# The key cache read in eight 4 MB transfers instead of sixteen 2 MB ones, through slots that keys and values share

## The chip, the cores and the metric

The kernel runs on one core of a Trainium2 chip. The metric is device time in microseconds (us), the median of several executions. One further execution is recorded by the hardware profiler; its times are of that one execution.

## The reference

One decode step for four sequences (batch B = 4, one new token each, width 576): a normalised input goes through an attention branch over a sliding window of a key and value cache, and through an MLP branch, and the two results and the input are added.

```python
x = A_x
xn = _layernorm(x)
return x + _A_ref(xn, A_k_cache, A_v_cache, A_wq, A_wo) + _B_ref(xn, B_w1, B_w2, B_w3, B_w4)

def _A_ref(x, k_cache, v_cache, wq, wo):     # caches: (4, 16 kv heads, 8192, 128)
    q = (x @ wq).reshape(B, 1, 32, 128).transpose(0, 2, 1, 3)
    k = repeat(k_cache[:, :, Sk - 2048:, :], 2)   # the last 2048 rows; 2 query heads per kv head
    v = repeat(v_cache[:, :, Sk - 2048:, :], 2)
    p = softmax(einsum("bhqd,bhkd->bhqk", q, k) * 128 ** -0.5)
    return einsum("bhqk,bhkd->bhqd", p, v).reshape(B, 1, 32 * 128) @ wo

def _B_ref(x, w1, w2, w3, w4):               # w1, w2: 576x576; w3: 576x4608; w4: 4608x576
    h = gelu(layernorm(x) @ w1)
    hs = concat(shifted quarters of h) @ w2  # with one token the shifted quarters are zero
    x1 = x + hs
    return x1 + gelu(layernorm(x1) @ w3) @ w4
```

All inputs are bf16. The windows of keys (K) and values (V) are 33.55 MB each; the weights make up the rest of the 88.5 MB that are read.

## The kernel before

**Transfers.** SyncE (SP) issues all large transfers, in the order of their keys, each after its waits (`add_dma`, L205): wq, w1, w2, w3, the first part of w4, then K0 to K15, V0 to V7, the rest of w4, and wo in five pieces. SP waits at the head of its list, so a transfer whose wait is open holds back those behind it.

**Storage.** `kring` holds four slots of 16 KB per partition for K, one 2 MB transfer each (`kslot`). `vring` holds five times 16 KB. V comes in 4 MB transfers; its four slots (`vslot`) are the two halves of `vring`'s first 64 KB and the two halves of `kring`. Before the loops the same memory holds weights: wq in the upper half of `kring`, w3 and the first part of w4 in `vring`. At the end wo goes to `vring`.

**K.** Transfer c brings four kv heads of one sequence, 2048 rows of 128 elements each (`CH`, `kv_src`). The 128 partitions are 32 groups of 64 consecutive rows times 4 heads, the row groups outermost; a partition gets one run of 16 KB. K0 and K1 have no wait, K2 waits for `q` (wq has been used), and from K4 on transfer c waits until TensorE has transposed all of transfer c - 4 (`t_done`).

TensorE runs a loop of `N_LOOP` = 4 turns over `N_CB` = 4 chunks (one chunk is one transfer). A chunk has 8 blocks. For each block `emit_T` (L508) makes eight 128x128 transposes into one of four PSUM buffers, with a permutation `perm_bf` as the moving operand that sorts the columns by head; VectorE or ScalarE copies the buffer to one of 16 `ktb` buffers (L492, L491, five and three of eight blocks). Two blocks into the next chunk, `emit_SC` (L515) makes 16 score matmuls of 512 columns: per matmul the right side is one head's columns of two `ktb` buffers (16 row groups of 32 consecutive elements), the left side a padded block of q (`Qs`, which VectorE copies from `Qpad` for each chunk). All chunks add into the same four PSUM banks `Sps`, [128, 4, 512].

**Between.** After the last chunk: row maximum (L521), exponential (L525), a transpose on VectorE (L543), and 64 small matmuls with selection matrices `pick_bf` (L537) that bring the probabilities into V's order; `mH_bf` spreads them by head (L568).

**V.** Transfer c holds a quarter of the window of two sequences, all 16 heads, in runs of 32 KB per partition with sequence and head outermost (`v_src`). The first MLP output `MO0` (L399, 48 matmuls on w4) stands in V0's list of waits, since `vring` held w3 and w4. V2 and V3 wait for K chunks (`kring` becomes free), and V4 to V7 for the V matmuls of the transfer that used the slot before (`PV`, L576; 64 matmuls per transfer). The last transfer is cut in two halves. The pieces of wo wait for the V matmuls of V4 and V5.

**The end.** The result is normalised, transposed and multiplied by wo piece by piece as it lands (L399), then copied out.

Of the kernel before, what the change touches and what calls it, by code (L numbers as in the profile page):

```python
# [6 lines left out]
BF16 = mybir.dt.bfloat16  # L7
# [7 lines left out]
N_LOOP = 4  # L15
N_CB = 4
# [21 lines left out]
def bass_parallel_sum__sliding_block_cached__mixer_s_mlp__decode_kernel(  # L38
# [8 lines left out]
    NU = 4  # L47
    NC = B * Hkv // NU
    NI = 128 // NU
    NT = W // NI  # L50
    UE = NT * Dh
    NBLK = NT // 8
    NB = NC * NBLK
    LB = N_CB * NBLK
    assert N_LOOP * N_CB == NC and LB % 4 == 0 and LB % NKT == 0
# [6 lines left out]
    CH = [(b, gq) for gq in range(4) for b in range(B)]  # L62
    VCH = [(bp, qt) for bp in range(NPAIR) for qt in range(NVS)]
    NCV, NTV = len(VCH), 2 * NT
# [6 lines left out]
    with ExitStack() as ctx:  # L71
        def sb(name, shape, dt):
            return ctx.enter_context(nc.sbuf_tensor(name, shape, dt))
# [7 lines left out]
        PT_t = sb("PT", [128, NT * 32], BF16)  # L81
# [13 lines left out]
        wot = lambda a, n: vring[:, wo_at(a):wo_at(a) + n * D].rearrange("p (r n) -> p r n", r=n)  # L95
# [39 lines left out]
        Qs = sb("Qs", [128, N_CB, 128], BF16)  # L135
# [46 lines left out]
        for j in range(LB):  # L182
            S["E", j] = sem(f"evac{j}")
# [32 lines left out]
        for n in range(NB):  # L216
            j = n % LB
            ev_val[f"E{n}"] = (("E", j), n // LB + 1 + (j >= LB - 4))
# [26 lines left out]
        pool_ident(permT_bf, "permT_bf", [[-1, NI], [-NI, NU]], permT_bf[:].rearrange("p (i u) -> p i u", u=NU), -93)  # L245
        P(lambda e: e.memset(ktb[:, NKT // 2 * 1024:NKT * 1024], 0.0), key=-92, inc=(("E", LB - 2), 1))  # L246
        P(lambda e: e.memset(Qs[:, N_CB - 1, :], 0.0), key=-91, inc=(("E", LB - 1), 1))
        for j in (LB - 4, LB - 3):
            P(lambda e, j=j: e.sem_inc(S["E", j], 1), key=-90)
# [7 lines left out]
        for gl in range(2):  # L257
            for x in range(2 * NVS):
                v = pick_bf[:, x, gl, 16 * gl:16 * gl + 16].rearrange("p (u r) -> p u r", u=NU)
                P(lambda e, v=v, x=x: e.affine_select(out=v, in_=v, compare_op=ALU.is_equal, fill=0.0, base=-(8 * (x // 2) + x % 2),  # L260
                                                      pattern=[[-NI, NU], [-2, 4]], channel_multiplier=1),
                  waits=["pick11"], sig=f"pick2{gl}{x}", key=-84 + 0.1 * (8 * gl + x))
# [31 lines left out]

        t_done = lambda c: f"T{NBLK * c + NBLK - 1}"
        for c in range(NC):
            w = [t_done(c - N_CB)] if c >= N_CB else (["q"] if c >= 2 else [])
            add_dma([(kslot(c % N_CB), kv_src(A_k_cache, c))], ("k", c % N_CB), w, c)
        for c in range(NCV):
            w = [f"PV{2 * (c - NVS) + 1}"] if c >= NVS else [t_done(NC - N_CB + 2 * c - 3)] if c >= 2 else ["MO0"]  # L300
            for n, (u0, u1) in enumerate([(0, NH), (NH, NTV)] if c == NCV - 1 else [(0, NTV)]):
                add_dma([(vslot(c % NVS)[:, Dh * u0:Dh * u1], v_src(c, u0, u1))], ("v", c % NVS, n), w, KS + c + 0.1 * n)
# [191 lines left out]
        for n in range(NB):  # L494
            c, k = n // NBLK, n % NBLK
            if k == 0:
                add("dve", lambda e, c=c: e.tensor_copy(out=Qs[:, c % N_CB, :], in_=Qpad_t[:, 128 * (4 * CH[c][0] + CH[c][1]):][:, 0:128]),
                    waits=["qT15"] + ([f"SC{c - N_CB}"] if c >= N_CB - 1 else []), key=n)
            eng, f = evac(n)
            w = [f"T{n}"] + ([f"SC{c - 2}"] if c >= 1 else [])  # L500
            add(eng, f, waits=w + (["hT", "hs1", "h2_2"] if n == 0 else []), key=n + 0.2, inc=(("E", n % LB), 1))

        def emit_T(e, j, wait):
            k, kb = j // NBLK, j % NBLK
            wait(j)
            ins = None
            for t in range(8):
                ins = e.transpose(tb[j % 4][:, t, :], kslot_t(k)[:, 8 * kb + t, :], perm_bf[:])  # L508
            ins.then_inc(S["T"], 1)

        def emit_SC(e, k):
            ins = None
            for q in range(4):
                for u in range(NU):
                    ins = e.matmul(Sps[32 * u:32 * u + 32, q, :].rearrange("p (t i) -> p t i", t=16),  # L515
                                   lhsT=Qs[:, k, 32 * u:32 * u + 32], rhs=ktgrp[:, (4 * k + q) % (NKT // 2), :, u, :],
                                   start=False, stop=False, tile_position=(0, 32 * u), skip_group_check=True)
            return ins
# [25 lines left out]
        for qt in range(4):  # L544
# [6 lines left out]
            else:  # L551
# [8 lines left out]
        add("dve", lambda e: e.tensor_copy(out=rinvB[:].rearrange("p (c u e) -> p c u e", u=NU, e=2),  # L560
                                           in_=rinvps.rearrange("p (u c e) -> p c u e", u=NU, e=2)),
# [10 lines left out]
        def emit_PV(e, k, h):  # L572
            ins = None
            for g in range(NH // 2):
                t = NH * h + 2 * g
                ins = e.matmul(ps[:, 0, 0:256], lhsT=PTpad[:, 2 * (k % 2) + h, 2 * g:2 * g + 2].rearrange("p t h e -> p (t h e)"),  # L576
                               rhs=vslot(k)[:, Dh * t:Dh * (t + 2)], start=(k == 0 and t == 0), stop=(k == NVS - 1 and t == NTV - 2),
                               skip_group_check=True)
            ins.then_inc(S["PV"], 1)
# [99 lines left out]
        with nc.Fori(0, N_LOOP, engines=[PE], head_slot={PE: 0}) as it:  # L679
            turn = e.snap(it + 1)  # L680
            landed = e.snap(16 * it + 16)

            def wait(j):
                if j % NBLK == 0:
                    e.wait_ge(S["k", j // NBLK], landed)
                e.wait_ge(S["E", (j - 4) % LB], turn)
            for j in range(LB):
                emit_T(e, j, wait)
                if j % NBLK == 2:
                    k = (j // NBLK - 1) % N_CB  # L690
                    e.wait_ge(S["E", NBLK * k + 6], turn)
                    e.wait_ge(S["E", NBLK * k + 7], turn)
                    emit_SC(e, k).then_inc(S["SC"], 1)
# [50 lines left out]
```

## Time and profile before

| | |
|---|---|
| median of 3 runs | 214.64 us (214.55 to 214.80) |
| span of the profiled execution (first to last instruction) | 213.5 us |
| data read from HBM | 88.49 MB, 415 GB/s over the span |
| TensorE matmuls / weight loads busy | 170.0 / 131.6 us |
| VectorE / ScalarE busy | 119.2 / 59.8 us |
| mean granted TensorE clock | 0.942 |

The profile gives no device time of its own for the profiled execution beside its span; the runs' median is 1.1 us above the span, which is the start and the end outside the first and last instruction. An engine's busy time is a sum over the whole span. Landing times can be read from the chain that ended last, where a DMA piece ends when its transfer has landed, and from TensorE's timeline where a group of matmuls starts after a wait for a DMA.

### The profile page before, as it was taken

To read this page: it belongs to the slowest core of one execution; us is meant where nothing else is said; L and a number is where in the kernel's file an instruction comes from. 1 tells how busy PE (TensorE), PEld (TensorE's weight loads), DVE (VectorE), ACT (ScalarE), POOL (GpSimd) and SP (SyncE) were. 2 spreads that over 40 slices of the span, in tenths; PEclk is the share of its full clock that TensorE was granted. 3 is DMA by queue.
4 is the path that set the end of the run, shared out by engine and by line. 5 is a ranking of instruction groups with operands and counts; after the bars stand their busy time and mean duration, and the time that the engine had idled before them with its cause. 6 is when DMAs were issued, how large, how long until landed. Compare 5 with 4: busy or idle time off the path is not lost.

```text
span 213.5 us, 4894 instructions
## 1 busy us (share of the span) xinstructions
PE 170.0 (80%) x2207; PEld 131.6 (62%) x2211; DVE 119.2 (56%) x185; ACT 59.8 (28%) x72; POOL 16.3 (8%) x39
## 2 busy tenths in 40 slices
PE   2028268579999999999999913899999768599965
PEld 0013115338778888887888702598888658488732
DVE  4973700017776777777677756999674572600110
ACT  2001212005665666666566655100000000000000
POOL 8992000000000000000000000000000000000000
PEclk9999857679999999999999995999999999999999
DMA  7999989999999999999999999999999999999992
GB/s 277 411 380 507 428 369 428 428 430 418 439 414 424 430 433 427 424 436 430 422 424 473 411 448 418 421 461 404 442 424 414 461 411 442 393 436 421 430 417 108
DMA packets 5795, 88.66 MB, mean 415 GB/s; under 512 B 652, under 2 KB 1048, under 8 KB 1816
## 3 DMA queue, kind: packets, MB, share of 16 engines
q1 hardware_dynamic: 5768, 88.49, 97.5%
q8 instruction: 8, 0.13, 0.2%
q14 instruction: 3, 0.02, 0.0%
q10 hardware_dynamic: 16, 0.01, 0.0%
HBM read 88.49 MB, written 0.00 MB: 415 GB/s over the span
## 4 chain that ended last, share of the span: by engine, by line
DMA 47%; PE 44%; DVE 4%; SPq 2%; issue 1%; ACT 1%
PE ps L508 23%; DMA vring<-in_B_w_dram 16%; DMA vring<-in_A_wo_dram 13%; DMA vring<-in_A_v_cache_dram 12%; PE ps L576 10%; DMA kring<-in_A_k_cache_dram 7%; PE ps L515 6%; PE ps L399 3%; SPq L205 2%; DVE vring L543 1%; DVE rmax L521 1%; DVE ktb L568 1%; PE ps L537 1%; ACT ktb L491 0%; PE ps L345 0%
## 5 line engine op out<-in xcount | busy, mean ns | idle before, releaser
L492 DVE COPY ktb<-ps 128x1024 bf16<-128x1024 bf16 x80 | 53.8, 689 | 22.1 <-PE ps L508 22.1
L508 PEld LDWEIGHTS ps<-perm_bf,kring 128*128 128x128 bf16 x1024 | 57.4, 98 | 8.7 <-issue 8.3
L508 PE MATMUL ps<-perm_bf,kring 128*128 128x128 bf16 x1024 | 60.6, 219 | 1.1 <-issue 1.1
L491 ACT ACTIVATE ktb<-ps 128x1024 bf16<-128x1024 bf16 x48 | 47.7, 1023 | 30.2 <-PE ps L508 30.1
L568 DVE TENSOR_TENSOR ktb<-PT,mH_bf 128x4096 bf16<-128x4096 bf16 x16 | 36.2, 2287 | 13.3 <-PE ps L576 13.3
L576 PE MATMUL ps<-vring,ktb 128*128 128x256 bf16 x256 | 28.6, 273 | 4.6 <-DMA vring<-in_A_v_cache_dram 3.8
L576 PE MATMUL ps<-kring,ktb 128*128 128x256 bf16 x256 | 28.6, 273 | 2.6 <-DMA kring<-in_A_v_cache_dram 2.6
L576 PEld LDWEIGHTS ps<-vring,ktb 128*128 128x128 bf16 x256 | 24.8, 98 | 7.9 <-issue 3.6
L576 PEld LDWEIGHTS ps<-kring,ktb 128*128 128x128 bf16 x256 | 25.0, 98 | 6.1 <-issue 2.8
L635 ACT ACTIVATE out_sb<-ps 4x288 bf16<-4x288 f32 x1 | 0.4, 402 | 76.7 <-PE ps L399 76.7
L515 PE MATMUL ps<-ktb,Qs 128*32 128x512 bf16 x272 | 17.8, 382 | 1.2 <-ACT ktb L491 1.2
L335 PE MATMUL ps<-ident_bf,xn_bf 4*128 4x4 bf16 x8 | 0.6, 170 | 11.8 <-DVE xnT L352 9.0
L594 DVE TENSOR_SCALAR tmp<-ps,maskd 128x128 f32<-128x128 f32 x2 | 0.7, 350 | 16.5 <-PE ps L576 16.5
L515 PEld LDWEIGHTS ps<-ktb,Qs 128*32 128x32 bf16 x272 | 5.7, 95 | 6.7 <-DVE ktb L492 1.3
L399 PE MATMUL ps<-vring,h2T_sb 128*4 128x288 bf16 x72 | 7.7, 390 | 2.3 <-DMA vring<-in_B_w_dram 2.3
L537 PE MATMUL ps<-vring,pick_bf 128*32 128x256 bf16 x64 | 3.9, 411 | 6.4 <-DVE rinv L555 6.4
L335 PEld LDWEIGHTS ps<-ident_bf,xn_bf 4*128 4x128 bf16 x8 | 0.4, 112 | 12.8 <-DVE xnT L352 9.1
L325 DVE TENSOR_SCALAR xn_bf<-xn_bf,mv,rstd 4x576 bf16<-4x576 bf16 x1 | 7.5, 7473 | 0.0
L399 PEld LDWEIGHTS ps<-vring,h2T_sb 128*4 128x4 bf16 x72 | 3.9, 110 | 5.6 <-DMA vring<-in_B_w_dram 2.5
L537 PEld LDWEIGHTS ps<-vring,pick_bf 128*32 128x32 bf16 x64 | 2.1, 121 | 8.2 <-DVE rinv L555 6.9
L246 POOL MEMSET ktb<- 128x8192 bf16 x1 | 6.9, 6925 | 0.0
L399 PE MATMUL ps<-vring,ORT 128*4 128x288 bf16 x64 | 4.6, 286 | 2.4 <-DMA vring<-in_A_wo_dram 2.2
(115 smaller groups left out, 84.2 us busy)
## 6 DMA issues: line engine op xcount, KB each, us to landing
kring<-in_A_k_cache_dram SPq DMA_DIRECT2D x16, 2048.0 KB, 13.2
vring<-in_A_v_cache_dram SPq DMA_DIRECT2D x4, 4096.0 KB, 24.5
kring<-in_A_v_cache_dram SPq DMA_DIRECT2D x3, 4096.0 KB, 33.8
vring<-in_B_w_dram SPq DMA_DIRECT2D x1, 4608.0 KB, 24.5
kring<-in_A_wq_dram SPq DMA_DIRECT2D x1, 4096.0 KB, 12.2
kring<-in_A_v_cache_dram SPq DMA_DIRECT2D x2, 2048.0 KB, 27.7
vring<-in_B_w_dram SPq DMA_DIRECT2D x1, 3456.0 KB, 34.4
vring<-in_A_wo_dram SPq DMA_DIRECT2D x1, 1872.0 KB, 30.6
```

Source lines behind the costliest of these rows:

```text
L205: e.dma_start(o_, i_).then_inc(S[skey], 16)
L246: P(lambda e: e.memset(ktb[:, NKT // 2 * 1024:NKT * 1024], 0.0), key=-92, inc=(("E", LB - 2), 1))
L325: add("dve", lambda e: e.tensor_scalar(out=dst[:], in0=src[:], scalar1=mv[:, idx, 0:1], scalar2=rstd[:, idx:idx + 1], op0=ALU.subtract, op ...
L399: return e.matmul(ACC[h], lhsT=lhsT, rhs=rhs, start=start, stop=stop, tile_position=(0, 32 * h), skip_group_check=True)
L491: return "act", lambda e: e.activation(out=ktbuf[:, n % NKT], in_=tb[n % 4], func=ACTF.Copy)
L492: return "dve", lambda e: e.tensor_copy(out=ktbuf[:, n % NKT], in_=tb[n % 4])
L508: ins = e.transpose(tb[j % 4][:, t, :], kslot_t(k)[:, 8 * kb + t, :], perm_bf[:])
L515: ins = e.matmul(Sps[32 * u:32 * u + 32, q, :].rearrange("p (t i) -> p t i", t=16), lhsT=Qs[:, k, 32 * u:32 * u + 32], rhs=ktgrp[:, (4 * k ...
L521: add("dve", lambda e: e.tensor_reduce(out=rmax[:], in_=Sps, axis=AX.XY, op=ALU.max), waits=["SCend"], sig="rmax", key=KS)
L537: ins = e.matmul(ps[32 * j:32 * j + 32, 4 + qt, 256 * ih:256 * (ih + 1)].rearrange("p (t a e) -> p t a e", a=NPAIR, e=2), lhsT=pick_bf[:, ...
L568: return lambda e: e.tensor_tensor(out=PTpad[:, n % 4], in0=PTv[:, qt, NH * h:NH * (h + 1), bp, :].unsqueeze(2).to_broadcast([128, NH, NX, ...
L576: ins = e.matmul(ps[:, 0, 0:256], lhsT=PTpad[:, 2 * (k % 2) + h, 2 * g:2 * g + 2].rearrange("p t h e -> p (t h e)"), rhs=vslot(k)[:, Dh * ...
```

## The change

K comes in eight transfers of 4 MB: eight kv heads of one sequence, 16 row groups of 128 consecutive rows times 8 heads, the row groups outermost, so that a partition gets one run of 32 KB. Four slots of 32 KB per partition (`slot`: the two halves of `kring`, then of `vring`'s first 64 KB) serve K0 to K7 in turn and then V0 to V7. K1 now waits for `q`, K2 for `MO0` (K2 and K3 go into `vring`), K4 to K7 for the transposes of the transfer four before, and V0 to V3 for those of K4 to K7. wo goes to `kring`, where V4 and V5 were.

A chunk is still 8 blocks of transposes and 16 score matmuls, but now half a transfer; the loop has eight chunks and runs twice. Since 32 semaphores (`NE`) for the copies serve 64 blocks of a turn, the value that is waited for changes in the middle of the body. A score matmul takes one head's columns of four `ktb` buffers: 32 row groups of 16 consecutive elements; two banks of `Sps` are written per chunk. `Qs` is copied once per transfer, 256 wide. `perm_bf`, `permT_bf` and `pick_bf` have new patterns for the new order, with the same number of instructions.

```diff
-N_LOOP = 4
-N_CB = 4
+N_LOOP = 2
+N_CB = 8
+NE = 32
...
-    NU = 4
-    NC = B * Hkv // NU
+    NU = 8
+    NCK = B * Hkv // NU
     NI = 128 // NU
     NT = W // NI
-    UE = NT * Dh
-    NBLK = NT // 8
+    NC = 2 * NCK
+    UE = NT * Dh // 2
+    NBLK = NT // 16
...
-    CH = [(b, gq) for gq in range(4) for b in range(B)]
+    CH = [(b, gh) for gh in range(2) for b in range(B)]
...
-        kslot = lambda s: kring[:, s * UE:(s + 1) * UE]
-        kslot_t = lambda s: kslot(s).rearrange("p (t d) -> p t d", t=NT)
-        vslot = lambda k: (vring, vring, kring, kring)[k][:, k % 2 * 2 * UE:(k % 2 + 1) * 2 * UE]
+        slot = lambda k: (kring, kring, vring, vring)[k][:, k % 2 * 2 * UE:(k % 2 + 1) * 2 * UE]
+        slot_t = lambda k: slot(k).rearrange("p (x t d) -> p x t d", x=2, t=NT // 2)
...
-        ktgrp = ktb[:].rearrange("p (s t u i) -> p s t u i", s=NKT // 2, t=16, u=NU)
+        ktgrp = ktb[:].rearrange("p (s t u i) -> p s t u i", s=NKT // 4, t=32, u=NU)
...
-        wot = lambda a, n: vring[:, wo_at(a):wo_at(a) + n * D].rearrange("p (r n) -> p r n", r=n)
+        wot = lambda a, n: kring[:, wo_at(a):wo_at(a) + n * D].rearrange("p (r n) -> p r n", r=n)
...
-        def kv_src(cache, c):
-            b, gq = CH[c]
-            return cache[b, NU * gq:NU * gq + NU, Sk - W:Sk, :].rearrange("g (i t) d -> i g (t d)", t=NT)
+        def k_src(c):
+            b, gh = CH[c]
+            return A_k_cache[b, NU * gh:NU * gh + NU, Sk - W:Sk, :].rearrange("g (i t) d -> i g (t d)", t=NT)
...
-        t_done = lambda c: f"T{NBLK * c + NBLK - 1}"
-        for c in range(NC):
-            w = [t_done(c - N_CB)] if c >= N_CB else (["q"] if c >= 2 else [])
-            add_dma([(kslot(c % N_CB), kv_src(A_k_cache, c))], ("k", c % N_CB), w, c)
+        t_done = lambda c: f"T{2 * NBLK * (c + 1) - 1}"
+        for c in range(NCK):
+            w = [t_done(c - NVS)] if c >= NVS else ([], ["q"], ["MO0"], [])[c]
+            add_dma([(slot(c % NVS), k_src(c))], ("k", c % NVS), w, c)
         for c in range(NCV):
-            w = [f"PV{2 * (c - NVS) + 1}"] if c >= NVS else [t_done(NC - N_CB + 2 * c - 3)] if c >= 2 else ["MO0"]
+            w = [f"PV{2 * (c - NVS) + 1}"] if c >= NVS else [t_done(NCK - NVS + c)]
...
-            if k == 0:
-                add("dve", lambda e, c=c: e.tensor_copy(out=Qs[:, c % N_CB, :], in_=Qpad_t[:, 128 * (4 * CH[c][0] + CH[c][1]):][:, 0:128]),
-                    waits=["qT15"] + ([f"SC{c - N_CB}"] if c >= N_CB - 1 else []), key=n)
+            if k == 0 and c % 2 == 0:
+                add("dve", lambda e, c=c: e.tensor_copy(out=Qs[:, c // 2 % 2, :],
+                                                        in_=Qpad_t[:, 128 * (4 * CH[c // 2][0] + 2 * CH[c // 2][1]):][:, 0:256]),
+                    waits=["qT15"] + ([f"SC{c - 3}"] if c >= 2 else []), key=n)
...
-                ins = e.transpose(tb[j % 4][:, t, :], kslot_t(k)[:, 8 * kb + t, :], perm_bf[:])
+                ins = e.transpose(tb[j % 4][:, t, :], slot_t(k)[:, t % 2, 4 * kb + t // 2, :], perm_bf[:])
...
-            for q in range(4):
-                for u in range(NU):
-                    ins = e.matmul(Sps[32 * u:32 * u + 32, q, :].rearrange("p (t i) -> p t i", t=16),
-                                   lhsT=Qs[:, k, 32 * u:32 * u + 32], rhs=ktgrp[:, (4 * k + q) % (NKT // 2), :, u, :],
+            for q in range(2):
+                for g in range(NU):
+                    u = g % 4
+                    ins = e.matmul(Sps[32 * u:32 * u + 32, 2 * (k % 2) + q, :].rearrange("p (t i) -> p t i", t=32),
+                                   lhsT=Qs[:, k // 2 % 2, 32 * g:32 * g + 32], rhs=ktgrp[:, 2 * (k % 2) + q, :, g, :],
...
         with nc.Fori(0, N_LOOP, engines=[PE], head_slot={PE: 0}) as it:
-            turn = e.snap(it + 1)
+            turn = [e.snap(2 * it + 1), e.snap(2 * it + 2)]
             landed = e.snap(16 * it + 16)
 
             def wait(j):
-                if j % NBLK == 0:
-                    e.wait_ge(S["k", j // NBLK], landed)
-                e.wait_ge(S["E", (j - 4) % LB], turn)
+                if j % (2 * NBLK) == 0:
+                    e.wait_ge(S["k", j // (2 * NBLK)], landed)
+                e.wait_ge(S["E", (j - 4) % NE], turn[j // NE])
```

More of the change, by code (lines that the diff above doesn't have):

```diff
@@ L181, in bass_parallel_sum__sliding_block_cached__mixer_s_mlp__decode_kernel @@
         S["SC"] = sem("score")
-        for j in range(LB):
+        for j in range(NE):
             S["E", j] = sem(f"evac{j}")
@@ L244, in bass_parallel_sum__sliding_block_cached__mixer_s_mlp__decode_kernel @@
         pool_ident(perm_bf, "perm_bf", [[-1, NU], [-NU, NI]], perm_bf[:].rearrange("p (u i) -> p u i", u=NU), -94)
[L245 to L248, printed above, removed]
+        pool_ident(permT_bf, "permT_bf", [[-1, 32], [-32, 4]], permT_bf[:].rearrange("p (i u) -> p i u", u=4), -93)
+        P(lambda e: e.memset(ktb[:, NKT // 2 * 1024:NKT * 1024], 0.0), key=-92, inc=(("E", NE - 2), 1))
+        P(lambda e: e.memset(Qs[:, 1, :], 0.0), key=-91, inc=(("E", NE - 1), 1))
+        for j in (NE - 4, NE - 3):
             P(lambda e, j=j: e.sem_inc(S["E", j], 1), key=-90)
```

38 lines of the change are left out of this document (19 added, 19 removed).

## The prediction

> **What bounds the kernel now.** I read the page first: the engines' busy shares, the row of DMA engines, the queues and the issues.
>
> ```profile
> span 213.5 us, 4894 instructions
> PE 170.0 (80%) x2207; PEld 131.6 (62%) x2211; DVE 119.2 (56%) x185; ACT 59.8 (28%) x72; POOL 16.3 (8%) x39
> DMA  7999989999999999999999999999999999999992
> q1 hardware_dynamic: 5768, 88.49, 97.5%
> q8 instruction: 8, 0.13, 0.2%
> kring<-in_A_k_cache_dram SPq DMA_DIRECT2D x16, 2048.0 KB, 13.2
> ```
>
> No compute engine is full. The 16 DMA engines are: from the second slice to the last but one their row holds nines and one eight, and queue 1, which carries all data, fills 97.5% of 16 engines' span. The time is therefore the time to move 88.5 MB, plus a start and an end. An edit that shortens TensorE's work gains nothing, and one that lengthens it costs nothing until the queue runs dry.
>
> Second, the chain that ended last, in order of time (start, length, what). Its DMA pieces end where a transfer landed.
>
> ```profile
> 5.03 34.43 DMA vring<-in_B_w_dram
> 39.50 5.92 PE ps L399 x48
> ...
> 47.45 1.51 PE ps L508 x24
> 48.97 0.98 PE ps L515 x16
> 49.94 3.71 PE ps L508 x64
> ...
> 103.76 13.99 DMA kring<-in_A_k_cache_dram
> ...
> 122.67 1.03 ACT ktb L491
> ...
> 136.40 7.16 PE ps L576 x64
> ...
> 150.74 25.78 DMA vring<-in_A_v_cache_dram
> 176.52 0.14 issue
> 176.66 7.16 PE ps L576 x64
> 183.82 0.02 issue
> 183.83 27.01 DMA vring<-in_A_wo_dram
> ```
>
> The first w4 part landed at 5.03 + 34.43 = 39.46, the sixteenth K transfer at 103.76 + 13.99 = 117.75, V5 (counted from V0) at 176.52, the wo piece that the chain ends with at 183.83 + 27.01 = 210.84. The PE pieces in between come from waits that link the chain; the transfers queued behind one another kept running under them.
>
> Third, TensorE's timeline where it waits for V, and the windows of the K and V stretches (columns: length, busy time of PE, PEld, DVE, ACT, POOL, clock, DMA share, GB/s).
>
> ```profile
> 166.85 7.16 PE L576 MATMUL ps<-vring,ktb 128*128 128x256 bf16 x64 [1.30 <-DMA vring<-in_A_v_cache_dram]
> ...
> 176.66 7.15 PE L576 MATMUL ps<-vring,ktb 128*128 128x256 bf16 x64 [2.48 <-DMA vring<-in_A_v_cache_dram]
> 186.37 7.15 PE L576 MATMUL ps<-kring,ktb 128*128 128x256 bf16 x64 [2.56 <-DMA kring<-in_A_v_cache_dram]
> ```
>
> ```profile
> 39.46:117.75 78.29, 77.03 (x1251) 62.13 (x1252) 51.57 (x91) 43.97 (x45) 0.00 (x0) 0.96 1.01 428
> 117.75:176.52 58.77, 46.62 (x489) 38.72 (x490) 43.22 (x36) 9.36 (x15) 0.00 (x0) 0.94 1.00 430
> ```
>
> Both stretches have full DMA engines. The K stretch moves sixteen 2 MB transfers in 78.29 us, 4.893 us each, so 9.786 us for 4 MB. The V stretch, 4 MB transfers whose rows are already 32 KB runs, shows what a 4 MB transfer costs: TensorE starts on V5 and V6, each at its landing, at 176.66 and 186.37, 9.71 us apart.
>
> **The transfers.** The bytes stay. K goes from sixteen transfers of 128 rows of 16 KB to eight of 128 rows of 32 KB. If they cost what V's cost, the K stretch is 8 x 9.71 = 77.7 us in place of 78.29: 0.6 us less. The other bound is the 16 KB price kept, nothing gained. I take V's price, the row of exactly this size and run length. The windows' 428 and 430 GB/s point the same way but are too coarse to size it, and the V stretch holds a slip: six V transfers at 9.71 are 58.3 us and it took 58.77.
>
> K's heads lie 8192 x 128 x 2 B = 2 MB apart. With eight heads per transfer two head rows are interleaved more closely than with four; V has its rows of 32 batch-heads outermost, all 2 MB apart, and runs at 430 GB/s all the same. So I charge nothing for the address pattern. [...]
>
> **Whether the queue ever runs dry.** Everything else is free as long as each transfer is issued before the one ahead of it lands; so I follow the schedule, with landings every 9.71 us from 39.46.
>
> - K0 lands at 49.2, K1 at 58.9, K7 at 117.1, V3 at 156.0. Before, K0's 2 MB landed about 44.4 and TensorE, ready at 47.45, did not wait. Now it starts at 49.2.
> - K2 and K3 go into vring, where w3 and w4 stood, and wait for MO0. MO0 ends at 39.50 + 5.92 = 45.4; K0 and K1 keep the engines busy until 58.9, a cover of 13 us. K1 waits for q in SP's queue; w3 and w4 are queued ahead of it, so nothing is short.
> - TensorE needs 3.71 + 0.98 = 4.69 us per 2 MB, 9.4 per 4 MB, less than 9.71: it waits for each K chunk. K4 is issued at 58.6 against 78.3 (K3's landing), V0 when K4 is transposed, about 97 against 117.
> - The last K chunk is now twice as large, so 4.7 us more work follow its landing. Before, from the landing (117.75) to the first V matmul (136.40) was 18.65; now 117.1 + 18.65 + 4.7 = 140.5. The first V is done at 147.6, and only then may V4 be issued. The queue runs dry at 156.0: a cover of 8.4 us, where before it was about 13. V5 to V7 follow at 7.2 us intervals against landings every 9.71, so the cover grows; TensorE has caught up by V5 or V6.
> - The wo pieces go to kring behind V4 and V5 (slots 0 and 1 as before), at about 176 and 183.5; V7 alone fills the engines until 194.8.
>
> So 4.7 us of added TensorE delay at the end of K is hidden under V0 to V3. Eight Qs copies fewer on VectorE, eight issues fewer on SP, other masks on GpSimd: all beside full DMA engines, nothing.
>
> **The score matmuls** read ktb in runs of 16 elements rather than 32. Rows for runs of other lengths:
>
> ```profile
> 123.83 1.05 PE L515 MATMUL ps<-ktb,Qs 128*32 128x512 bf16 x16 [1.21 <-ACT ktb L491]
> 131.29 3.89 PE L537 MATMUL ps<-vring,pick_bf 128*32 128x256 bf16 x64 [6.41 <-DVE rinv L555]
> ```
>
> L515, with runs of 32, takes about 61 ns per 512 columns; L537, with runs of 2, 61 ns per 256. So the bounds are 1 and 2 times. 16 is nearest to 32: I take 1, and the doubling is a rival.
>
> **Instruction fetch.** The K loop's body doubles: 512 transposes and 128 score matmuls, run twice. Queue 8 carries instructions over the same DMA engines; I read it as TensorE's program, since its packets come with the first pass of TensorE's loops.
>
> ```profile
> q1 hardware_dynamic: 2273, 33.47, 100.6%
> q8 instruction: 4, 0.07, 0.3%
> ...
> q1 hardware_dynamic: 1737, 29.67, 100.8%
> q14 instruction: 1, 0.01, 0.0%
> ```
>
> The first pair is the DMA view of 39.46 to 117.75, the second of 67 to 136: four blocks in the loop's first pass or just behind it, none in the three later ones. So a body of 320 matmuls stays resident. The program's matmuls, each counted once, are 2207 less three quarters of L508's 1024 and of 256 of L515's, less half of L576's 512: 991, over 8 blocks, 124 a block. 320 more are two or three blocks. Four blocks in the K stretch took 0.3% of 16 x 78.29 us = 3.8 us of engine time, about 0.9 us each, on one engine. What that costs the whole depends on the engine it meets. A transfer has landed when the last of the engines has done its share, so only a block on the latest engine moves the landings; and the V slip, which came before 166.85, is not made up afterwards (the landings stay 9.71 apart). Four blocks left the K rate even; of the three in the V stretch one may be its slip of 0.5. So 0 to 0.9 us for a block, and I take 0, because most of the 16 engines are not the latest.
>
> **Sum.** -0.6 for the transfers, 0 for all else. The span becomes 212.9. The profiled execution's span is 213.5 and the runs' median 214.64, so 1.1 us lies around the span, which the change leaves: 214.05 us. Telling it from no change needs about 0.2% of this kernel, 0.43 us.
>
> **Rivals.**
>
> 1. An added instruction block meets the DMA engine that is already last: 0.9 us for one, 1.8 for two, less the 0.6. 214.9 to 215.9, and 215.4 in the middle, slower. For it: two or three more blocks, and the V slip shows that such a thing is seen. Against: sixteen engines. The point of decision is one engine. If the longer body (640 matmuls, five blocks by 124 a block) does not stay resident, five more blocks come on the second pass and the chance rises; what TensorE itself would wait, about 0.9 us for a block at the branch, lies under the cover of 8.4. [...] 0.25 together.
> 2. The 16 KB and 32 KB prices are equal for K's address pattern: 214.65, no change. Against it: V's row. 0.13.
> 3. The score matmuls double to 1.95 us per half chunk. TensorE then needs 11.3 us per K chunk, ends K at 139.6 in place of 126, starts V at about 154.3 and V4 is issued at 161.4, 5.4 us after the queue ran dry: 219.4. It decides from about 1.6 us per half chunk. 0.04.
> 4. K's rows, two heads of which are now read at a time, slow one another. Each per cent costs 0.78 us of the K stretch: at 0.8% the gain is gone, at 1.3% the kernel is slower by 0.2%, at 5% it takes 218. V's rate, with more such rows, is against it. 0.03. [...]
>
> That the change does not happen is excluded: SP's list has eight K transfers of 128 x 16384 elements.
>
> **Numbers.** The forecast has 0.55: 214.05, its own range 213.7 (most of the V slip falls on another engine this time) to 214.35 (half of the transfers' gain is lost). Faster by over 0.2% is that case less a little of its upper end: 0.54. Same: rival 2, that end and rival 1's lower edge, 0.16. Slower: the rest of rival 1 and rivals 3 and 4, 0.30. The range 213.7 to 215.6 leaves out rivals 3 and 4 and the top of 1.
>
> **What would show it.** Right: K7 lands near 117.1 and each K landing 9.71 after the last; TensorE's loop shows a wait of 0.3 us per chunk; the first V matmul near 140.5; SP issues V4 near 147.6; V landings stay 9.71 apart; queue 8 has 10 or 11 packets; the last wo lands 0.6 earlier. Wrong: a gap in the row of DMA engines near 156, a score group above 1.6 us, K landings at 9.79 or more, queue 8 with 15 or more packets, or V and wo landings slipping by about 1 us once.

## The result, and the profile after

| | before | after |
|---|---|---|
| median of 4 runs each | 214.72 us (214.55 to 215.79) | 297.88 us (296.63 to 299.10) |
| ratio after / before | | 1.3865, 95% interval 1.3814 to 1.3915 |
| the profiled execution, its span | 214.80 us, 213.5 | 298.05 us, 296.8 |

The changed kernel is 83.2 us slower. The forecast was 214.05 us with a range to 215.6: wrong in sign and by two orders of magnitude in size.

The page of the changed kernel, the rows that answer to those shown of before:

```profile
span 296.8 us, 4864 instructions
PE 188.4 (63%) x2207; PEld 143.3 (48%) x2211; DVE 119.4 (40%) x177; ACT 60.3 (20%) x72; POOL 16.4 (6%) x39
PEclk9998777569579588596695975966958999999999
DMA  8999999999999999999999999999999999999992
GB/s 301 407 455 427 416 233 210 212 205 216 220 212 214 212 214 212 208 219 212 212 212 212 216 218 212 212 243 442 426 424 435 433 423 428 433 417 432 419 419 82
q1 hardware_dynamic: 4616, 88.49, 97.5%
q8 instruction: 11, 0.18, 0.3%
kring<-in_A_k_cache_dram SPq DMA_DIRECT2D x4, 4096.0 KB, 64.8
```

The DMA row is a row of nines as before, and queue 1 fills the same 97.5% of 16 engines. By these two rows nothing has changed; the queue never ran dry. The row below tells another story: from the sixth slice to the 27th the same busy engines move 205 to 243 GB/s, about half of what they move before and behind. The bytes are the same 88.49 MB.

The windows of the K and the V stretch of the changed kernel (columns: length, busy time of PE, PEld, DVE, ACT, POOL, clock, DMA share, GB/s):

```profile
42.58:200.28 157.70, 86.58 (x1171) 67.61 (x1172) 48.61 (x79) 42.61 (x43) 0.00 (x0) 0.74 1.00 214
200.28:279.38 79.10, 69.83 (x715) 58.31 (x718) 50.65 (x41) 11.29 (x17) 0.00 (x0) 0.91 1.00 428
```

K moves at 214 GB/s and V, in transfers of the same size and run length, at 428, both with a DMA share of 1.00. K's stretch takes 157.70 us where 77.7 were forecast.

TensorE's timeline of the changed kernel (start, length, what, and in brackets the wait before it):

```profile
81.74 2.74 PE L510 MATMUL ps<-perm_bf,kring 128*128 128x128 bf16 x24 [8.87 <-DMA kring<-in_A_k_cache_dram]
84.41 1.47 PE L518 MATMUL ps<-ktb,Qs 128*32 128x512 bf16 x16
...
89.50 1.05 PE L518 MATMUL ps<-ktb,Qs 128*32 128x512 bf16 x16
...
101.49 2.74 PE L510 MATMUL ps<-perm_bf,vring 128*128 128x128 bf16 x24 [8.61 <-DMA vring<-in_A_k_cache_dram]
...
200.33 2.74 PE L510 MATMUL ps<-perm_bf,vring 128*128 128x128 bf16 x24 [8.89 <-DMA vring<-in_A_k_cache_dram]
...
225.65 7.16 PE L579 MATMUL ps<-kring,ktb 128*128 128x256 bf16 x64 [0.49 <-DVE ktb L571]
```

TensorE starts on a new K transfer at 81.74, 101.49 and, six transfers behind the first of these, at 200.33: 19.75 and, over all six, 19.77 us apart where the forecast had 9.71. Each time it has waited 8 to 9 us for the transfer. So K is bound by its transfers, each at twice its price. TensorE's granted clock (the page's PEclk row) drops to 5 to 7 tenths in many slices of K; it waits there anyway.

The first and the last DMA piece of the chain that ended last (start, length, what):

```profile
5.01 37.57 DMA vring<-in_B_w_dram
...
270.16 24.01 DMA kring<-in_A_wo_dram
```

The last wo landed at 294.17, before at 210.84. Of these 83.3 us, 3.1 lie ahead of K (the first w4 part landed at 42.58 in place of 39.46; by the trace's semaphore updates the first of the 16 engines had done its share at 37.6, before at 37.7, but the last one 5.0 us after it in place of 1.8; K0 is then already under way on the engines that are done, which I take for the reason and did not test), 79.4 in the K stretch (157.70 in place of 78.29), and 0.8 from K7's landing to the end (93.9 in place of 93.1).

### The profile page after: what moved, and what is told of

Read it like the earlier page. It is cut to its first block, busy times and chain, and to the rows that moved or that the text cites. A ratio compares the mean times of both kernels' runs of the same rounds, so it can differ in the third digit from the quotient of the medians.

```text
span 296.8 us, 4864 instructions
## 1 busy us (share of the span) xinstructions
PE 188.4 (63%) x2207; PEld 143.3 (48%) x2211; DVE 119.4 (40%) x177; ACT 60.3 (20%) x72; POOL 16.4 (6%) x39
## 3 DMA queue, kind: packets, MB, share of 16 engines
q1 hardware_dynamic: 4616, 88.49, 97.5%
HBM read 88.49 MB, written 0.00 MB: 298 GB/s over the span
## 4 chain that ended last, share of the span: by engine, by line
PE 49%; another core or an unknown queue 24%; DMA 21%; DVE 3%; SPq 1%; issue 1%; ACT 1%
PE ps L510 24%; PE ps L579 14%; DMA vring<-in_B_w_dram 13%; DMA kring<-in_A_wo_dram 8%; PE ps L518 7%; PE ps L400 2%; SPq L206 1%; DVE vring L546 1%; DVE rmax L524 1%; DVE ktb L571 1%; PE ps L540 1%; ACT ktb L492 0%; PE ps L346 0%; PE ps L590 0%
## 5 line engine op out<-in xcount | busy, mean ns | idle before, releaser
L510 PE MATMUL ps<-perm_bf,kring 128*128 128x128 bf16 x512 | 36.3, 239 | 36.8 <-DMA kring<-in_A_k_cache_dram 36.8
L510 PE MATMUL ps<-perm_bf,vring 128*128 128x128 bf16 x512 | 35.9, 238 | 34.1 <-DMA vring<-in_A_k_cache_dram 34.1
L510 PEld LDWEIGHTS ps<-perm_bf,kring 128*128 128x128 bf16 x512 | 33.8, 108 | 41.6 <-issue 25.2
L510 PEld LDWEIGHTS ps<-perm_bf,vring 128*128 128x128 bf16 x512 | 33.4, 108 | 39.8 <-issue 22.4
L518 PE MATMUL ps<-ktb,Qs 128*32 128x512 bf16 x272 | 22.8, 468 | 1.2 <-ACT ktb L492 1.2
L518 PEld LDWEIGHTS ps<-ktb,Qs 128*32 128x32 bf16 x272 | 6.5, 109 | 9.7 <-issue 5.3
## 6 DMA issues: line engine op xcount, KB each, us to landing
vring<-in_B_w_dram SPq DMA_DIRECT2D x1, 3456.0 KB, 37.6
```

Source lines behind the costliest of these rows:

```text
L510: ins = e.transpose(tb[j % 4][:, t, :], slot_t(k)[:, t % 2, 4 * kb + t // 2, :], perm_bf[:])
L518: ins = e.matmul(Sps[32 * u:32 * u + 32, 2 * (k % 2) + q, :].rearrange("p (t i) -> p t i", t=32), lhsT=Qs[:, k // 2 % 2, 32 * g:32 * g + 3 ...
```

## The experiments

### 1. The transfers alone

What was open: why does K's transfer cost twice V's, with the same size, the same runs and the same queue? The first kernel holds nothing but loads, thirteen patterns of four transfers each, from HBM into a fresh buffer, each pattern after the one before it has landed. "Outermost" is the first dimension of the source as the transfer names it, with its count; 16 outermost with 8 within is written 16 x 8:

```
four_16k   K of the kernel before: 4 heads x 32 groups of 64 rows, 2 MB        "g (i t) d -> i g (t d)"
eight_32k  K of the kernel after: 8 heads x 16 groups of 128 rows, 4 MB        "g (i t) d -> i g (t d)"
eight_32k_v   the same from V's cache
vorder_k   V's order (32 heads outermost, 4 groups) from K's cache
headsout_32k  8 heads outermost, 16 groups within                              "g (i t) d -> g i (t d)"
pair_2m, pair_4m, pair_16m   16 outermost, 8 blocks within, 0.5, 1 or 4 MB apart (the name: blocks four apart)
skew_4k    as eight_32k with the heads 4 KB less than 2 MB apart
four_32k   4 heads x 32 groups of 128 rows (4096 rows)
eight_16k  8 heads x 16 groups of 64 rows (1024 rows), 2 MB
four_half16k, whole_32k   as four_16k, every second run; 2 whole heads, 64 groups each
```

> This kernel only loads: twelve patterns, four transfers each, nothing is computed and the output is zeros. Theory A (two rows of heads 8 MB apart, read side by side by different DMA engines, halve each other): the changed kernel's pattern (eight_32k) gives about 214 GB/s from K and from V alike, also in 16 KB runs (eight_16k); four heads, row groups outermost, at 32 KB pitch (four_32k) give about 430, and the order with heads outermost (headsout_32k) and V's order read from K (vorder_k) give about 430; the distance of the pair (2, 4, 8, 16 MB) says which bits of the address matter, and eight heads with a pitch 4 KB short of 2 MB (skew_4k) give about 430. Theory B (rows 32 KB apart read side by side halve each other, heads do not matter): four_32k and four_half16k (16 KB runs at 32 KB pitch) fall to about 214 too, and skew_4k stays at 214. Theory C (not the loads but what the kernel does beside them): all twelve at 425 to 435 GB/s.

The DMA issues of this kernel (pattern, engine, count, KB of one, median us from issue to landing). All four of a pattern are issued at once, so the median is about two and a half transfers and a start of some 2 us:

```profile
eight_32k<-in_A_k_cache_dram SPq DMA_DIRECT2D x4, 4096.0 KB, 51.2
vorder_k<-in_A_k_cache_dram SPq DMA_DIRECT2D x4, 4096.0 KB, 26.5
eight_32k_v<-in_A_v_cache_dram SPq DMA_DIRECT2D x4, 4096.0 KB, 51.2
...
pair_2m<-in_A_k_cache_dram SPq DMA_DIRECT2D x4, 4096.0 KB, 51.7
...
pair_16m<-in_A_k_cache_dram SPq DMA_DIRECT2D x4, 4096.0 KB, 51.5
skew_4k<-in_A_k_cache_dram SPq DMA_DIRECT2D x4, 4096.0 KB, 51.8
four_32k<-in_A_k_cache_dram SPq DMA_DIRECT2D x4, 4096.0 KB, 26.0
whole_32k<-in_A_k_cache_dram SPq DMA_DIRECT2D x4, 4096.0 KB, 26.0
four_16k<-in_A_k_cache_dram SPq DMA_DIRECT2D x4, 2048.0 KB, 13.8
eight_16k<-in_A_k_cache_dram SPq DMA_DIRECT2D x4, 2048.0 KB, 26.1
```

From one landing to the next, eight_32k takes 19.7 to 19.9 us, as in the kernel; vorder_k, four_32k and whole_32k 9.63 to 9.77; four_16k 4.83 to 5.0 for its 2 MB and eight_16k 9.76 to 9.84. The slow price thus needs no other work around it. It comes with either cache, with the eight blocks 0.5, 1, 2 or 4 MB apart or 4 KB off 2 MB, and with runs of 16 KB as of 32 KB. None of the theories in the expectation holds as it was put. All that the slow ones share is 16 as the outermost count, with 8 blocks within; the fast ones have 32 there, except whole_32k, which is written 2 x 64 but reads 128 rows that follow one another.

headsout_32k, with 8 outermost, is slower still. The windows of eight_32k, vorder_k and headsout_32k in the same kernel (columns: length, DVE, POOL, clock, DMA share, GB/s; each window holds some 2 us of start):

```profile
22.90:104.80 81.90, 0.00 (x0) 0.00 (x0) 1.00 0.97 205
104.80:146.90 42.10, 0.00 (x0) 0.00 (x0) 1.00 0.94 399
...
229.00:385.00 156.00, 0.00 (x0) 0.00 (x0) 1.00 0.50 111
```

With 16 outermost all engines are busy and the rate is half; with 8 outermost half of the engines' time is used and the rate is a quarter. The records of single packets show why the quarter: a 32 KB packet takes 1.21 us in vorder_k and 2.53 in eight_32k (medians), and 2.53 in headsout_32k too, so that pattern has the slow packets on half of the engines.

### 2. The kernel with the heads outermost

The changed kernel with K's rows in V's kind of order, heads outermost, and the column order of the transposes to match:

```diff
-        pool_ident(perm_bf, "perm_bf", [[-1, NU], [-NU, NI]], perm_bf[:].rearrange("p (u i) -> p u i", u=NU), -94)
+        pool_ident(perm_bf, "perm_bf", [[-1, 128]], perm_bf[:], -94)
...
-            return A_k_cache[b, NU * gh:NU * gh + NU, Sk - W:Sk, :].rearrange("g (i t) d -> i g (t d)", t=NT)
+            return A_k_cache[b, NU * gh:NU * gh + NU, Sk - W:Sk, :].rearrange("g (i t) d -> g i (t d)", t=NT)
```

> The changed kernel with one difference: the rows of a K transfer stand heads outermost (partition = 16 x head + row group), and the permutation of the transposes is the identity. Theory A and B (the address pattern of the loads is at fault): K transfers land 9.7 us apart, and the time is what the prediction gave without the pattern, 214.0 to 214.4 us, or up to 1 us more if the added instruction blocks meet the last DMA engine. Theory C (the sharing of slots, the longer loop or the larger chunk is at fault): about 298 us as before.

Six runs took 436.51 to 467.32 us, against 214.68 for the kernel before: even the shortest is far from both expected times. A stretch of the profiled execution (458.47 us) inside its K loop (columns as in the windows of the changed kernel):

```profile
44.00:190.00 146.00, 38.19 (x516) 29.33 (x512) 21.16 (x35) 18.49 (x19) 0.00 (x0) 0.63 0.50 113
```

113 GB/s at a DMA share of 0.50: the loads-only pattern's rate (111 and 0.50), in the kernel. "V has heads outermost and is fast" was the wrong lesson from V's row; V has 32 of them outermost and 428 GB/s, and 8 are a quarter as fast. The trace's semaphore updates go with the DMA shares: eight behind the first one for a transfer of headsout_32k, at a share of 0.50, and 16 in all for one of eight_32k, at 0.97. I read this as 8 engines at work in the one and 16 in the other; why the 16 move half of V's rate these numbers do not say.

### 3. Where the rows land

Four heads in 16 groups of 128 rows fill 64 partitions. The second loads-only kernel puts them on partitions 0 to 63 (`low`) or 64 to 127 (`high`), issues the two halves from two queues at once (`split`) or one after the other (`alternate`), sends both queues to partitions 0 to 63 (`lowlow`), and adds 64 groups of 2 (`two_32k`) and 32 groups of 4 in two 16 KB runs (`double_16k`).

```
low       buf[0:64, ...]   <- 16 groups x 4 heads, from SyncE
high      buf[64:128, ...] <- the same
split     buf[0:64, ...]   from SyncE and buf[64:128, ...] from ScalarE's queue
lowlow    buf[0:64, ...]   from SyncE and from ScalarE's queue
alternate buf[0:64, ...]   then buf[64:128, ...], both from SyncE
double_16k  "(g x) (i t) d -> i (g x) (t d)", x=2, t=64
```

> Loads alone again, ten patterns, output zeros. In the first of these runs eight heads by 16 row groups ran at half rate whatever the distance of the heads, and heads outermost at a quarter; four heads by 32 row groups ran full. [...] Theory E (the rows read side by side from HBM are at fault): split stays at 215, low and lowlow may be anything. [...]

Measured from landing to landing: low and high 10.0 to 10.25 us for 2 MB, half rate each; alternate 9.94 for 2 MB, half; lowlow by its window 196 GB/s, half; two_32k 9.67, four_32k 9.68 and double_16k 9.71 for 4 MB, full rate. Both halves at once from two queues, the window of `split` (columns as in experiment 1):

```profile
210.00:289.50 79.50, 0.00 (x0) 0.00 (x0) 1.00 0.97 211
```

211 GB/s, which is what E expects (215). For a cause in the partitions that are written I had expected 350 to 430 for two queues, and that failed; the third kernel asks the same in another way. What this one gives is a layout that is fast: double_16k.

The third kernel tells these two causes apart with a destination that straddles the halves. `mid_64` writes the very same rows to partitions 32 to 95; `blocks_16x8`, `blocks_32x4` and `blocks_64x2` read nearly contiguous rows, with one row left out behind each block so that the counts stay as they are named.

```
low_64   buf[0:64, ...]    <- 16 groups x 4 heads
mid_64   buf[32:96, ...]   <- the same
high_64  buf[64:128, ...]  <- the same
blocks   rows[0:i * (g + 1)].rearrange("(i y) n -> i y n", y=g + 1)[:, 0:g]
```

> Loads alone, seven patterns, output zeros. [...] low_64, mid_64 and high_64 read the very same rows (four heads, 16 row groups, 2 MB) into partitions 0 to 63, 32 to 95 and 64 to 127. [...] Theory E (the source rows): all three 205. [...] eight_32k is the control at 213.

Its windows, in the order low_64, mid_64, high_64, blocks_16x8, blocks_32x4, blocks_64x2, eight_32k (columns as in experiment 1):

```profile
1.00:43.97 42.97, 0.14 (x1) 0.00 (x0) 1.00 0.95 195
43.97:66.02 22.05, 0.00 (x0) 0.00 (x0) 1.00 0.90 380
66.02:108.94 42.92, 0.00 (x0) 0.00 (x0) 1.00 0.94 195
108.94:192.00 83.06, 0.00 (x0) 0.00 (x0) 1.00 0.97 202
192.00:234.10 42.10, 0.00 (x0) 0.00 (x0) 1.00 0.94 399
234.10:276.20 42.10, 0.00 (x0) 0.00 (x0) 1.00 0.94 399
276.20:359.00 82.80, 0.00 (x0) 0.00 (x0) 1.00 0.97 203
```

From landing to landing mid_64 takes 4.83 us for the 2 MB that take 10.24 on partitions 0 to 63 and 10.2 on 64 to 127. A 32 KB packet takes 1.21 us in mid_64 and 2.57 in low_64 (medians). The rows and their order are the same; the destination alone differs. E, which looked for the cause in the source rows and had 205 GB/s for all three, falls. And 16 blocks of 8 nearly contiguous rows are as slow (19.97 us) as the kernel's K, 32 of 4 and 64 of 2 fast (9.66): with the addresses side by side the split alone decides.

Shown, then: on 128 partitions the rate hangs on the split (16 x 8 at 19.97 us against 32 x 4 at 9.66), on 64 with one and the same split on the partitions that are written (10.24 against 4.83), and in neither case on the source's addresses. Not shown: that the slow 16 x 8 comes from the partitions written as well, and how its rows are dealt to the engines, since the trace does not give that for a packet. Why 16 groups of eight take twice as long as 32 of four stays open.

### 4. The whole change at a full-rate split

Two kernels keep all else of the change (shared slots, eight 4 MB transfers, body of eight chunks) and alter the split. The first takes eight heads as 32 groups of 4 partitions, each with two 16 KB runs; its transposes and score matmuls read four heads per chunk, in runs of 32 elements, as before the change. It puts the head pairs in another order than the query padding assumes, so it computes other scores.

```diff
-            return A_k_cache[b, NU * gh:NU * gh + NU, Sk - W:Sk, :].rearrange("g (i t) d -> i g (t d)", t=NT)
+            return A_k_cache[b, 8 * gh:8 * gh + 8, Sk - W:Sk, :].rearrange("(g x) (i t) d -> i (g x) (t d)", x=2, t=NT // 2)
...
-                ins = e.transpose(tb[j % 4][:, t, :], slot_t(k)[:, t % 2, 4 * kb + t // 2, :], perm_bf[:])
+                ins = e.transpose(tb[j % 4][:, t, :], slot_t(k)[:, kb // 8, 8 * (kb % 8) + t, :], perm_bf[:])
...
```

> The changed kernel with K's 4 MB transfers laid out as 32 row groups by 4 partitions, two runs of 16 KB per partition; the transposes and score matmuls read four heads per chunk as in the kernel before. Which head's scores stand in which row is not the reference's; all else (eight transfers, shared slots, waits, loop run twice) is the changed kernel's. If the split alone is at fault, K transfers land 9.79 us apart (two times 4.893) and the time is 214.5 to 214.8 us, at most 1.3 us more if the added instruction blocks meet the last DMA engine; the first V matmul starts 4.7 us later than before and costs nothing. If the size of the transfer, the shared slots, the later V start or the longer loop is part of the loss, it stays above 217 us.

215.91 us (215.70 to 216.16), ratio 1.0048, 1.0031 to 1.0066. K's landings are 9.76 to 9.80 us apart, which is the 16 KB price of before, and the 83 us are gone. What is left is 1.2 us more than before.

The second changes one line, so that a transfer holds four heads in 32 groups of 128 rows, a 32 KB run each. It reads 4096 rows of half of the heads in place of the window's 2048 of all.

```diff
-            return A_k_cache[b, NU * gh:NU * gh + NU, Sk - W:Sk, :].rearrange("g (i t) d -> i g (t d)", t=NT)
+            return A_k_cache[b, 4 * gh:4 * gh + 4, Sk - 2 * W:Sk, :].rearrange("g (i t) d -> i g (t d)", t=NT)
```

> The changed kernel with one line different: a K transfer reads four heads by 32 row groups of 128 rows (4096 keys of four heads) in place of eight heads by 16 row groups, so the keys are not the window's; size (4 MB), runs (32 KB), number of transfers, slots, waits, loop and scores are the changed kernel's. [...] Sum 215.1 to 215.6 us. If the score matmuls in runs of 16 elements, the shared slots or the waits cost anything of their own, it is above 216; if K stays at 19.6 us per transfer, the row shape was not the cause.

215.40 us (215.24 to 215.97, twelve runs), before 214.59; ratio 1.0034, 1.0017 to 1.0051: inside what was expected with K at the prediction's 9.71 us and 1.2 us for the longer body. TensorE's timeline of this kernel, the last two K transfers and the first V matmul:

```profile
107.82 1.51 PE L510 MATMUL ps<-perm_bf,vring 128*128 128x128 bf16 x24 [0.31 <-DMA vring<-in_A_k_cache_dram]
109.27 1.05 PE L518 MATMUL ps<-ktb,Qs 128*32 128x512 bf16 x16
...
117.47 1.51 PE L510 MATMUL ps<-perm_bf,vring 128*128 128x128 bf16 x24 [0.16 <-DMA vring<-in_A_k_cache_dram]
...
140.71 7.16 PE L579 MATMUL ps<-kring,ktb 128*128 128x256 bf16 x64 [0.79 <-DVE ktb L571]
...
186.94 7.15 PE L579 MATMUL ps<-vring,ktb 128*128 128x256 bf16 x64 [1.76 <-DMA vring<-in_A_v_cache_dram]
```

And its K stretch in the windows (columns as for the changed kernel):

```profile
40.00:117.00 77.00, 72.35 (x1168) 58.46 (x1165) 47.54 (x77) 41.24 (x42) 0.00 (x0) 0.96 1.00 429
```

K at 429 GB/s, landings 9.70 to 9.72 apart but for one of 9.85. This one line is worth 297.88 less 215.40 = 82.5 us: the split, 16 x 8 in place of 32 x 4, is the cause of the slowdown.

### 5. The longer body alone

Both kernels of experiment 4 stay slower than before, by 1.2 and 0.8 us, with full-rate transfers. The kernel before, with only its K loop's body doubled (eight chunks, two turns; four K slots and sixteen 2 MB transfers as they were):

```diff
-N_LOOP = 4
-N_CB = 4
+N_LOOP = 2
+N_CB = 8
+NSL = 4
+NE = 32
...
-            add_dma([(kslot(c % N_CB), kv_src(A_k_cache, c))], ("k", c % N_CB), w, c)
+            add_dma([(kslot(c % NSL), kv_src(A_k_cache, c))], ("k", c % NSL), w, c)
...
```

> The kernel before with one difference: the K loop's body holds eight chunks and runs twice, as in the changed kernel; transfers, slots and scores are those of before. In the run with two 16 KB runs the last DMA engine fell 3.3 us behind the first, against 2.2 before, with 11 blocks of instructions on queue 8 against 8. If the longer program is the cause, this kernel has 11 blocks and takes 215.5 to 216.2 us; if it was the later start of V or the larger transfers, it takes 214.5 to 214.9.

215.95 us (215.84 to 216.24), before 214.69; ratio 1.0055, 1.0038 to 1.0072: 1.26 us for a longer body and nothing else. Its page and, below it, the end of its chain:

```profile
span 214.6 us, 4894 instructions
q8 instruction: 11, 0.18, 0.3%
```

```profile
186.62 25.36 DMA vring<-in_A_wo_dram
```

Queue 8 has 11 packets where the kernel before has 8, and the span is 214.6 in place of 213.5. K's landings are unchanged at 4.89 us for 2 MB, and the last wo lands at 211.98 in place of 210.84. The trace has 16 semaphore updates for each of these transfers, which I read as the ends of the 16 engines' shares. By them the engines finish the last wo transfer within 3.49 us of each other, in the kernel before within 2.18 (3.34 and 3.58 in the two kernels of experiment 4). The first engine is done at the same time, 208.8 in place of 209.0; a transfer has landed only with its last engine (in the kernel before, V5's 16 updates come from 174.34 to 176.52, and TensorE, which waits for V5, starts at 176.66).

The updates of the transfers in between show where the spread grows. Blocks of instructions start on queue 8 at 73.68 and 81.95, the two that the K stretch has more; the landings just ahead of them have the engines 1.97 us apart, those behind them 2.05. The step comes between the landings of V1 (137.33) and V2 (148.49): from 2.04 to 3.48, and so it stays to the end. In that stretch a block starts at 141.64. Fifteen of the ends keep their distance from the first one; the end that jumps was already some 1.9 us behind at V1. The kernels of experiment 4 have the step at V2 too, from 1.83 to 3.47 and from 2.10 to 3.63. The kernel before has blocks in its V stretch as well, at 136.08, 148.21 and 163.22, but its last engine moves there by 0.37 alone. So nearly all of the 1.26 us comes in one step, not as a price of 0.4 for each of three blocks.

That the time goes with the body's length is shown; that it is a block on an engine already behind rests on these spreads, as no kernel here had the body without its blocks. Whether more blocks make such a meeting likelier, or only deal the later ones to other engines, stays open: one longer body was run.

### 6. Less work on VectorE

Part of the change could have shortened something of its own: it has eight Qs copies fewer on VectorE. The kernel before with all 16 of them, and four more of the copies that empty the transposes' PSUM buffers, moved to ScalarE:

```diff
-            if n % 8 in ACT_EVAC:
+            if n % 8 in ACT_EVAC or n in (27, 59, 91, 123):
...
-                add("dve", lambda e, c=c: e.tensor_copy(out=Qs[:, c % N_CB, :], in_=...),
+                add("act", lambda e, c=c: e.activation(out=Qs[:, c % N_CB, :], in_=..., func=ACTF.Copy),
```

> The kernel before with twenty instructions moved from VectorE to ScalarE (the sixteen Qs copies and four of the evacuations), nothing else. In the run with the longer loop body three more blocks of instructions cost 1.2 us; this is the opposite direction. The trace of before has three blocks on queue 14, at 28.5, 102.9 and 148.4 us; by the count of VectorE's instructions the first and last are VectorE's, and in the landings of before the engine that is last at the end (2.18 us behind the first) is one that was delayed at both times, the next one is 1.82 behind. If blocks on the last engine set the end, the block at 148.4 disappears and the time falls by about 0.35 us, to 214.2 to 214.5. If they do not, or if the block comes all the same, it stays at 214.6 to 214.8.

214.71 us against 214.69 over twelve runs, ratio 1.0003, 0.9985 to 1.0020. The expected gain of 0.35 us did not show; it lies at the edge of the interval, whose lower end is 0.32 us below no change. The device times can't tell a smaller gain from none. The trace shows that the block at 148.4 did go (queue 14 has 2 packets in place of 3) and that the engines end 1.96 us apart in place of 2.18; the spans of all runs have a mean of 213.26 against 213.40. So a gain of some 0.14 us may be there, less than half of what was expected. That twenty instructions fewer on VectorE change so little agrees with the prediction's reading that its work lies beside full DMA engines.

## Why the prediction was wrong

**The transfers: the step that failed.** The prediction took V's price of 9.71 us for K's new transfers as "the row of exactly this size and run length". Size and run length do not fix the price. V has 32 rows of batch-heads outermost, K after the change 16 row groups, and the prediction names the 32 as a matter of addresses alone, without asking what the count itself does. A K transfer took 19.77 us: (19.77 - 9.71) x 8 is 80 us, and the whole loss is 83. rows32, the same size and run length with 32 outermost, took 9.70 to 9.85; so the price was right for the shape it came from, and the sentence that carried it over was wrong. In the kernel before K's transfers had 32 outermost as V's have, so none of its rows for K or V priced 16; that should have been said as an open price.

**Rival 4** was the only one that let K's transfers grow dear, and it had 0.03. It was drawn as an effect of addresses, "two heads of which are now read at a time", and that mechanism is refuted: skew_4k, pair_16m and blocks_16x8 are as slow with other distances, and vorder_k is fast with its 32 heads 2 MB apart. Its price per cent holds (104% dearer at 0.78 us each makes 81 us), but no size was given that came near. The prediction set V's rate against it, "with more such rows"; but V's rows come as four neighbours from each of 32 heads, so V's rate did not price eight heads in 16 groups. What the runs show is that 4 KB off the 2 MB (skew_4k, 20.0 to 20.1 us) leave the transfer as slow as eight_32k (19.7 to 19.9). The two-sided bounds of this term, 9.71 and 9.786, were the prices of two rows of one and the same outermost count; a price for another shape was not bounded by them at all.

**The queue never dry: right.** With K at its forecast rate (rows32) the first V matmul came at 140.71 against 140.5 and V4 was issued at 147.90 against 147.6, and the DMA row of the changed kernel has no gap either. The slots shared by K and V, the later V4 and the larger last chunk cost nothing that can be seen: 214.05 of the forecast and the 1.26 of the longer body make 215.31, and rows32 took 215.40.

**The score matmuls: right.** A group of 16 takes 1.05 us with runs of 16 elements, as with runs of 32 before; rival 3 falls. The 1.47 at 84.41 follows a wait and a lower granted clock (0.74 over the stretch).

**The instruction blocks: right in number, wrong in price.** 11 packets on queue 8, as one of the two numbers given, and the doubled body stayed resident, as I read the trace of the changed kernel: a block starts on queue 8 at 128.68 and the next at 213.78, and the loop's second turn lies between them (K4 landed at 140.65, K7 at 200.28). The price was set to 0 "because most of the 16 engines are not the latest"; the longer body cost 1.26 us. The reasoning took each block alone against the one latest engine. By the spreads of experiment 5 an engine that has fallen behind stays behind (3.48 us at V2, 3.49 at the last transfer), so later blocks can find more than one engine that is nearly last (2.18 and 1.82 us behind the first at the end of the kernel before), and one block is enough: an engine some 1.9 us behind went to 3.48. The prediction's bound of 0.9 for a block is too small also: one step of the last engine was 1.4 to 1.6 us. V6 shows it in rows32: it is taken up at 186.94, though TensorE took up K7 at 117.47, 0.3 before its landing in the kernel before, where V6 was taken up at 186.37: 0.85 more from K7 to V6. Rival 1 had this mechanism, a block that meets an engine already last. That its middle, 215.4, is what rows32 measured is luck in part: it is the mean of one hit and two at 0.9 each, and the traces show one at more than that.

**The sum, put right.** 214.05 of the forecast, 1.26 for the longer body, 82.5 for the split into 16: 297.8, measured 297.88. The 82.5 are the difference from rows32, so this sum tests no more than the 215.31 above; taken by themselves, the eight transfers explain 80 of it, and some 3 lie ahead of K. Without the 16 x 8 split the change would still have been slower, 0.8 us in rows32, not faster.

No kernel of these experiments beats the kernel before. A split that takes eight heads of the 2048-row window in single 32 KB runs has only 16 groups of 128 rows for each head, so 16 or 8 outermost; with heads of two sequences outermost, as V does, there would be 32; such a load ran at full rate by itself (vorder_k, 9.63 to 9.77 us), but a kernel around it was not tried.

## What to carry to other kernels

Take a transfer's price from a row only if the whole shape agrees: the count of its outermost dimension (4 MB in 32 KB runs took 9.7 us with 32 and 19.8 with 16) and the destination's partitions (2 MB took 4.83 us on 32 to 95 and 10.24 on 0 to 63) as well as its size and run length. A row of DMA engines that shows nines says that they are occupied, not that they move data (here 214 GB/s in one stretch and 428 in the next, both with a share of 1.00): read the GB/s row of the same stretch beside it. And in a kernel whose DMA engines are full, a longer unrolled body need not be free: here it cost 1.26 us, most likely, by the spreads of the engines' ends, because an instruction block fell on a DMA engine that was already behind.

## What the runs showed of the hardware

- Loads of 128 partitions of 32 KB take 9.63 to 9.77 us with 32 or 64 outermost, 19.6 to 20.2 with 16, and 36.5 to 39.4 with 8. With 16 the DMA engines are shown busy all the time: in the changed kernel a 32 KB packet of K takes 2.51 us in the trace and one of V 1.22 (medians).
- The same 2 MB to 64 partitions took 4.83 us on partitions 32 to 95 and 10.24 us on 0 to 63.
- A DMA engine that had fallen behind did not catch up while the queue was full: in the kernel with the longer body the 16 engines' ends lay 3.48 us apart at V2 and 3.49 at the last transfer, some 60 us later.
- Two queues on the two halves of the partitions at once did not bring the rate back (211 GB/s, where 32 outermost from one queue had 399).
- After a wait of 8 to 9 us the first 24 transposes took 2.74 us in the changed kernel; in rows32, after waits of 0.2 to 0.3, 1.51. The granted clock of the two K stretches was 0.74 and 0.96.
